# A clamp for the weights' conversion, and five pieces of work put elsewhere in the steps of an attention and gated-product kernel

## The chip, the core and the metric

The kernel runs on one core of a Trainium2 chip. The core has a matrix engine (TensorE, PE in the profile; its weight loads are PEld), a vector engine (VectorE, DVE), a scalar engine (ScalarE, ACT), a general engine (GpSimd, POOL) and a queue engine that here only issues transfers (SyncE, SP). Each engine works through its own list of instructions in order, and waits on semaphores for the others. The metric is the time of one execution on the device in microseconds (us); the median of a few executions is given.

## The reference

```python
# x (8, 8, 512, 64) and state (8, 8, 32, 64) in float32; B, H, S, D = x.shape
scores = scale * x @ state.T                  # per batch and head: 512 x 32
a = softmax(scores);    xread = a @ state     # 512 x 64
scores2 = scale * state @ x.T                 # 32 x 512
a2 = softmax(scores2);  sread = a2 @ x        # 32 x 64
x = concat([xread, sread], axis=2)            # (8, 8, 544, 64)
x = x.transpose(0, 2, 1, 3).reshape(4352, 512)
h = x @ w_in                                  # w_in (512, 2048)
g = h * cos(h)
out = g @ w_out                               # w_out (2048, 512), out (4352, 512) in float32
```

The two weights arrive as 64-bit floating-point numbers, since numpy scaled them by a 64-bit scalar. The kernel has to bring them to 32 bits itself.

## The kernel before

**Tiles and steps.** The 8 batches have 512 token rows each. The work on tokens is cut into 128 steps: step 16b + f takes batch b and columns 128f to 128f + 127 of the hidden width 2048. Sixteen more steps (128 to 143) do all 256 state rows at once. In each step `hidden` (L467) fills a PSUM tile `h` with the hidden values, by two matmuls of 128x128 by 128x512; the profile counts two records for each. The attention is folded in: the left operand is `sw`, the product of state and `w_in` (`products`, L314, copied out of PSUM by `products_kept` on ACT or `products_taken` on DVE, L441), the right one is `aT`, the softmax. `h` comes in units of 2 pi.

**The gate** follows in four instructions. `gate` (L473, ACT) adds a large constant, which rounds; `gate2` (L476, DVE) subtracts it and `h`; `gate3` is Abs (L481, ACT) and Sin (L482, ACT), which gives the cosine; `gate4` (L488, DVE) multiplies with `h` into a slot of `g_all`. There are two `h` tiles, so `hidden` of step k can start only when `gate4` of step k - 2 is done.

**The second product** (`output`, L532) lags three steps behind, four in the first 16 steps. It treats two batches as a pair and uses seven instead of eight block products. For that `w_out` is cut into blocks `a11`, `a12`, `a21`, `a22`, from which POOL makes the sums `s1`, `s2`, `s4` and `s3` (L820; `s3` lies in the place of `a21`), eight instructions in the steps that `block_at` gives. In the second batch of a pair, differences of gated tiles are needed (`minus`, L494): for the first pair all on POOL, for later pairs one a step on DVE and, in the last eight steps of the pair, two on POOL. `s1` is read by outputs of steps 16 to 23, `s2` and `s4` by those of steps 24 to 31, `s3` by the outputs that one pair leaves to the next (`p7`).

**The conversion.** Each weight load (`loads`, 0 to 17, then 18 and 19, which fetch a part of `w_out` anew) goes through `convert_part`: "1" (ACT, L225) takes the high words as float32, without sign and times a power of two, "2" (ACT, L228) makes the three top bits of the low words; "b" (DVE, L231) shifts the former left by three; "c" (DVE, L234) puts the sign in; "d" (POOL, L239) adds the latter; "f" starts a later load on SP. Loads 0 to 3 are 128x512 values, the others 128x1024. `conv_at` gives the step in which "1" and "2" stand; the rest stands in the step after. Within a step the order written in the loop is the order on each engine: after `hidden` come `gate` and `gate2`, then the planned parts `go(1)` (ACT) and `go(3)` (DVE), then the conversions' DVE and POOL part, and "1" if ACT has no planned part; `gate3`; one instruction out of `later` (sums and transposes for the stores, L552, L559, on DVE); `gate4`; then the second halves `go(2)` (ACT) and `go(4)` (DVE) and "2".

**The plan.** `plan(b)` spreads the next batch's attention over a batch's steps: transposed tokens, `scores` (L314), `max1` (L328), `spread1` (L334), `shift` (L351), `max2` (L344), the exponentials (`exps`, L355 and L360, which need another table in ACT), the sums, the normalisation `norm1` (L381), then `turn` (PE, L387) with its eviction `turn_kept` (ACT, L392), `reads` (PE, L404) and `keep` (DVE, L414). `spread`, which `norm1` reads, and `a2T`, which `turn_kept` writes, are the same memory (`xT[:, 0:2]`). Before step 0 a stretch of instructions is written out by hand for batch 0.

Of the kernel before, what the change touches and what calls it, by code (L numbers as in the profile page):

```python
# [10 lines left out]
I32 = mybir.dt.int32  # L11
U32 = mybir.dt.uint32
ALU = mybir.AluOpType
ACTF = mybir.ActivationFunctionType
# [9 lines left out]
def kernel(  # L24
# [8 lines left out]
    nc = tc.nc  # L33
# [10 lines left out]
    scale = 1.0 / math.sqrt(D)  # L44
# [27 lines left out]
    a11, a12 = w_out[:, 0, 0:NH], w_out[:, 0, NH:NF]  # L72
# [3 lines left out]
    s3 = a21  # L76
# [128 lines left out]
    def convert(i, parts):  # L205

        for p in parts:  # L210
            if p == "f":
                if i not in (1, 2) and i + 3 < N_LOADS:
                    fetch(max(i + 4, 6))
            elif f64:
                convert_part(i, p)

    def convert_part(i, p):
        raw, dst = raws[i], loads[i][0]
        bits = dst.bitcast(I32)
# [3 lines left out]
        e = e.bitcast(I32)  # L223
        if p == "1":
            nc.scalar.activation(dst, raw.bitcast(F32)[:, :, :, 1],  # L225
                                 func=ACTF.Abs, scale=2.0 ** -112)
        elif p == "2":
            nc.scalar.activation(e, raw.bitcast(U32)[:, :, :, 0],  # L228
                                 func=ACTF.Copy, scale=2.0 ** -29)
        elif p == "b":  # L230
            nc.vector.tensor_scalar(bits, bits, 3, None,  # L231
                                    op0=ALU.logical_shift_left)
        elif p == "c":
            nc.vector.scalar_tensor_tensor(out=bits, in0=raw[:, :, :, 1],  # L234
                                           scalar=-2 ** 31, in1=bits,
                                           op0=ALU.bitwise_and,
                                           op1=ALU.bitwise_xor)
        else:
            nc.gpsimd.tensor_tensor(bits, bits, e, op=ALU.add)  # L239

# [478 lines left out]
    a0.all_tokens(3, 4)  # L719
    a0.scores()  # L720
    warm(10, acc[SIDE][1])
    convert(0, "12b")
    convert(1, "12")
    a0.max1()
    a0.spread1()
    a0.shift()
# [9 lines left out]
    convert(3, "12")  # L736
    a0.max2()
    a0.exp2()
    convert(2, "bcdf")

# [3 lines left out]
    def plan(b):  # L744
        pe, x_act, y_act, x_dve, y_dve = [
            {s: [] for s in range(NF)} for _ in range(5)]

        def prod(s, b, nt, *bank):
            pe[s].append((b, "products", nt) + bank)
            if b == 1 and nt > 0:  # L750
                x_dve[s].append((b, "products_taken", nt) + bank)
            else:
                x_act[s].append((b, "products_kept", nt) + bank)

        def pairs(s, b, name, kept, i):
            pe[s] += [(b, name, i), (b, name, i + 1)]
            x_act[s].append((b, kept, i))
            y_act[s].append((b, kept, i + 1))

        def early(b, s):  # L760
            if b == 1:
                pairs(s[0], b, "tokens", "tokens_kept", 0)
                pairs(s[1], b, "tokens", "tokens_kept", 2)
            else:
                for k in range(NK):
                    to = (x_dve, y_dve)[k % 2]
                    to[s[k // 2]].append((b, "tokens_turned", k))
            pe[s[2]].append((b, "scores"))
            x_dve[s[2]].append((b, "max1"))
            x_dve[s[3]].append((b, "spread1"))  # L770
            y_dve[s[3]].append((b, "shift"))
            x_dve[s[4]].append((b, "max2"))
            y_act[s[4]].append((b, "exps"))
            x_dve[s[5]].append((b, "sums"))
            y_dve[s[5]].append((b, "spread1"))
            x_dve[s[6]].append((b, "norm1"))

        def late(b, s):
            pairs(s[0], b, "turn", "turn_kept", 0)
            pe[s[1]].append((b, "reads", 0))  # L780
            pe[s[2]].append((b, "reads", 1))
            x_dve[s[2]].append((b, "keep"))
            if len(s) > 3:
                turned(b, s[3])

        def turned(b, s):
            pe[s].append((b, "keep2"))
            x_act[s].append((b, "keep3"))


        if b == 0:
            pe[0].append((0, "products", 0, SIDE, HC, WC))
            y_dve[0] += [(0, "products_taken", 0, SIDE, HC, WC),
                         (0, "inverse2")]
            prod(7, 0, 2, SIDE)
            prod(11, 0, 3)
            prod(13, 1, 0, MAIN)
            late(0, (1, 2, 3, 4))
            early(1, (5, 6, 7, 8, 9, 10, 11))
            late(1, (12, 13, 14))  # L800
        else:
            bank = (SIDE,) if b == 1 else ()
            if b == 1:
                turned(1, 0)
            prod(0, b, 1, *[MAIN for _ in bank])
            prod(4, b, 2, *bank)
            prod(9, b, 3, *bank)
            if b + 1 < B:
                prod(14, b + 1, 0)
                early(b + 1, (1 + (b == 1), 2 + (b == 1), 5, 6, 7, 8, 9))  # L810
                late(b + 1, (10, 11, 12, 15))
        return pe, x_act, y_act, x_dve, y_dve


    conv_at = {s: 4 + i for i, s in enumerate(
        (0, 1, 2, 3, 4, 5, 6, 7, 8, 10, 11, 12, 13, 14))}
    conv_at.update({B * NF + 5: N_LOADS, B * NF + 7: N_LOADS + 1})

    def blocks(op, out_, a, b, r):
        nc.gpsimd.tensor_tensor(out_[:, r], a[:, r], b[:, r], op=op)  # L820

    lo, hi = slice(0, NH // 2), slice(NH // 2, NH)
    block_at = {15: (ALU.add, s1, a21, a22, lo),
                17: (ALU.add, s1, a21, a22, hi),
                18: (ALU.subtract, s2, s1, a11, lo),
                19: (ALU.subtract, s2, s1, a11, hi),
                20: (ALU.subtract, s4, a12, s2, lo),
                21: (ALU.subtract, s4, a12, s2, hi),
                22: (ALU.subtract, s3, a11, a21, lo),
                23: (ALU.subtract, s3, a11, a21, hi)}  # L830
    LAG = 3

    line = []
# [1 line left out]
    for step, t in enumerate(all_tiles):  # L835
        s = step % NF
        if s == 0 and t.b < B:
            steps = plan(t.b)
        todo = [p[s] if t.b < B else [] for p in steps]

        def go(n):
            for p in todo[n]:
                part(*p)

        last, conv = conv_at.get(step - 1, -1), conv_at.get(step, -1)
        if step == B * NF + (0 if f64 else 8):
            fetch(N_LOADS + 2)
        if step == 4:
            warm(1, acc[MAIN][0])
        if step != 1:  # L850
            hidden(t)
        if step == 0:
            hidden(all_tiles[1])
            warm(3, acc[MAIN][0])
            gate(t)
            gate2(t)
            convert(3, "bcdf")
            convert(4, "1")
            go(0)
        else:  # L860
            go(0)
            if step == 5:
                states(1, acc[SIDE][1])
            gate(t)
            gate2(t)
            if step == 3:
                warm(4, acc[MAIN][0])
                part(0, "products", 1, SIDE)
                part(0, "products_kept", 1, SIDE)
            go(1)  # L870
            go(3)
            if step == 1:
                convert(4, "bcdf")
            elif last >= 0:
                convert(last, "bcdf")
            if conv >= 0 and not todo[1]:
                convert(conv, "1")
        gate3(t)
        if later:
            later.pop(0)()  # L880
        gate4(t)
        if conv >= 0 and todo[1] and step > 0:
            convert(conv, "1")
        if t.pair is not None:
            sums(t)
        if step == 6:
            states_kept(1, acc[SIDE][1])
        go(2)
        if conv >= 0:
            convert(conv, "2")  # L890
        go(4)
        if step in block_at:
            blocks(*block_at[step])
        if t.pair is not None:
# [36 lines left out]
```

## Time and profile before

| what | value |
|---|---|
| median of 3 runs (lowest, highest) | 786.97 us (786.81, 787.05) |
| the profiled execution | 786.81 us, its span in the profile 785.0 us |
| busy: PE, DVE, ACT, POOL | 765.1, 417.3, 389.1, 176.7 us |
| TensorE's granted clock | 1.00 in all stretches but the last 5 us |
| PE without a matmul, 0 to 65 us | 5.8 us |
| 65 to 103 us | 5.6 us |
| 103 to 190 us | 2.8 us |
| 190 to 506 us | 1.4 us, in two places |
| 506 to 785 us | 4.3 us, at the end |

The rows for PE without a matmul are the length of a stretch less PE's busy time in it. In a line of the order of time the first number is the start in us from the beginning of the span, the second how long the instruction, or a run of equal ones, was busy; then engine, line, operation, output and inputs with their shapes; in brackets stands how long the engine had been idle and what ended that. Such a run of equal instructions is marked x2, x4 and so on. A DVE instruction of 0.69 us lets the next one start after some 0.60 if that does not need its result.

### The profile page before, as it was taken

The numbers are of one execution on the slowest core, as the hardware profiler recorded it, in microseconds if no ns is written. First come the engines' busy times: TensorE is split into PE (matmuls) and PEld (weight loads), VectorE is DVE, ScalarE is ACT, GpSimd is POOL, SyncE is SP. The second block draws the span as 40 slices with busy tenths as digits, with TensorE's granted clock in tenths as the row PEclk, the third lists the DMA queues.
The fourth block names the chain that finished last, engine by engine and source line by source line (L and its number), as shares of the span: only waits on it lengthen the run. The fifth ranks groups of instructions, "written<-read, shape, count | busy, mean of one in ns | idle before, by whom it ended". The sixth has DMA issues, their size and how long they took to land.

```text
span 785.0 us, 7535 instructions
## 1 busy us (share of the span) xinstructions
PE 765.1 (97%) x2664; PEld 340.3 (43%) x2664; DVE 417.3 (53%) x656; ACT 389.1 (50%) x626; POOL 176.7 (23%) x118
## 2 busy tenths in 40 slices
PE   8998899899999999999999999999999999999997
PEld 3443433344344444444344434434444444455554
DVE  5768778623563466734554467635554446431431
ACT  3888954733463545633473446443563445322222
POOL 2344359673000000641000001640000004610200
PEclk9999999999999999999999999999999999999999
DMA  8595451060011510250104310330100114000021
GB/s 241 167 263 187 141 100 28 4 104 1 3 25 31 102 24 5 34 101 0 24 5 76 58 27 15 54 67 0 28 1 0 28 28 130 4 0 15 13 41 40
DMA packets 161957, 43.49 MB, mean 55 GB/s; under 512 B 153920, under 2 KB 153920, under 8 KB 161920
## 3 DMA queue, kind: packets, MB, share of 16 engines
q1 hardware_dynamic: 161024, 42.49, 24.8%
q10 hardware_dynamic: 768, 0.39, 0.2%
q8 instruction: 21, 0.34, 0.2%
q0 software_dynamic: 128, 0.13, 0.1%
q14 instruction: 16, 0.13, 0.1%
HBM read 34.08 MB, written 8.91 MB: 55 GB/s over the span
## 4 chain that ended last, share of the span: by engine, by line
PE 81%; ACT 10%; DVE 6%; issue 1%; DMA 1%; SPq 0%; POOL 0%; DVEq 0%
PE o L532 44%; PE h L467 26%; PE at L314 4%; PE o L652 4%; PE at L404 2%; ACT q L482 1%; ACT q L481 1%; ACT s L228 1%; DVE q L476 1%; ACT q L473 1%; DVE g_all L488 1%; ACT xT L360 1%; ACT w_in L225 1%; ACT L482 1%; DVE xT L334 1%
## 5 line engine op out<-in xcount | busy, mean ns | idle before, releaser
L467 PE MATMUL h<-aT,sw 128*128 128x512 f32 x512 | 241.5, 594 | 11.0 <-DVE g_all L488 8.1
L532 PE MATMUL o<-g_all,w_out 128*128 128x512 f32 x512 | 236.4, 598 | 1.2 <-POOL w_out L239 1.2
L494 POOL TENSOR_TENSOR g_all<-g_all 128x512 f32<-128x512 f32 x80 | 112.1, 1423 | 451.5 <-DVE g_all L488 447.9
L473 ACT ACTIVATE q<-h 128x512 f32<-128x512 f32 (+1 forms) x144 | 82.1, 570 | 262.3 <-PE h L467 262.2
L476 DVE SCALAR_TENSOR_TENSOR q<-q,h 128x512 f32<-128x512 f32 (+1 forms) x144 | 94.2, 654 | 216.9 <-ACT q L473 216.9
L532 PE MATMUL o<-g_all,s 128*128 128x512 f32 x384 | 177.3, 598 | 0.0
L488 DVE TENSOR_TENSOR g_all<-h,q 128x512 f32<-128x512 f32 (+1 forms) x144 | 94.8, 658 | 124.8 <-ACT q L482 118.6
L467 PEld LDWEIGHTS h<-aT,sw 128*128 128x128 f32 x512 | 96.4, 190 | 135.4 <-issue 110.7
L532 PEld LDWEIGHTS o<-g_all,w_out 128*128 128x128 f32 x512 | 94.0, 190 | 125.5 <-issue 118.4
L481 ACT ACTIVATE q<-q 128x512 f32<-128x512 f32 (+1 forms) x144 | 87.6, 608 | 93.5 <-DVE q L476 93.4
L532 PEld LDWEIGHTS o<-g_all,s 128*128 128x128 f32 x384 | 70.8, 190 | 91.7 <-issue 87.3
L482 ACT ACTIVATE q<-q,halfpi 128x512 f32<-128x512 f32 (+1 forms) x144 | 100.5, 698 | 4.5
L239 POOL TENSOR_TENSOR w_out<-w_out,s 128x1024 int32<-128x1024 int32 x10 | 23.9, 2390 | 77.1 <-DVE w_out L234 73.5
L494 DVE TENSOR_TENSOR g_all<-g_all 128x512 f32<-128x512 f32 x48 | 33.2, 692 | 1.6
L441 ACT COPY sw<-at 128x512 f32<-128x512 f32 x50 | 26.8, 589 | 9.0 <-PE at L314 9.0
L467 PE MATMUL h<-sT,w_in 128*128 128x256 f32 x128 | 30.2, 379 | 0.0
L652 PE MATMUL o<-w_out,g_all 128*128 128x512 f32 x64 | 29.6, 592 | 0.0
L467 PEld LDWEIGHTS h<-sT,w_in 128*128 128x128 f32 x128 | 24.3, 190 | 10.1 <-issue 6.7
L239 POOL TENSOR_TENSOR w_in<-w_in,s 128x1024 int32<-128x1024 int32 (+1 forms) x10 | 19.3, 1929 | 38.8 <-DVE w_in L234 36.5
L314 PE MATMUL at<-w_in,stT 64*32 64x512 f32 x400 | 27.2, 601 | 0.0
L538 DVE SCALAR_TENSOR_TENSOR held<-o,held 128x512 f32<-128x512 f32 x40 | 25.3, 675 | 2.9 <-PE o L532 2.9
L559 DVE STREAM_TRANSPOSE ot<-held 128x512 f32<-128x512 f32 x32 | 22.1, 692 | 0.0
(80 smaller groups left out, 427.7 us busy)
## 6 DMA issues: line engine op xcount, KB each, us to landing
out_dram<-ot SPq DMA_DIRECT2D x132, 64.0 KB, 2.0
g_all<-in_moe_w_out_dram SPq DMA_DIRECT2D x8, 1024.0 KB, 4.9
g_all<-in_moe_w_in_dram SPq DMA_DIRECT2D x6, 1024.0 KB, 5.2
xT<-in_x_dram SPq DMA_DIRECT2D x96, 64.0 KB, 2.3
x_b<-in_x_dram SPq DMA_DIRECT2D x24, 256.0 KB, 4.6
x_b<-in_x_dram SPq DMA_DIRECT2D x16, 128.0 KB, 4.0
g_all<-in_moe_w_in_dram SPq DMA_DIRECT2D x4, 512.0 KB, 6.0
x_b<-in_moe_w_out_dram SPq DMA_DIRECT2D x1, 1024.0 KB, 5.9
```

Of the source, the lines that this page charges most:

```text
L239: nc.gpsimd.tensor_tensor(bits, bits, e, op=ALU.add)
L314: nc.tensor.matmul(out=(to or at)[j][Ns * k:Ns * k + Ns, 0:n], lhsT=w[D * j:D * j + D, self.b, Ns * k:Ns * k + Ns], rhs=r(slice(D * j, D * ...
L441: (copy or nc.scalar.copy)(sw_of[self.b, nt][:, j, c0:c1], to[j][:, 0:c1 - c0])
L467: nc.tensor.matmul(out=t.hp, lhsT=t.lhs(i), rhs=t.rhs(i), start=(i == 0), stop=(i == t.kn - 1))
L473: nc.scalar.activation(t.q, t.hp, func=ACTF.Copy, bias=MAGIC)
L476: nc.vector.scalar_tensor_tensor(out=t.q, in0=t.q, scalar=MAGIC, in1=t.hp, op0=ALU.subtract, op1=ALU.subtract)
L481: nc.scalar.activation(t.q, t.q, func=ACTF.Abs)
L482: nc.scalar.activation(t.q, t.q, func=ACTF.Sin, bias=halfpi, scale=-TWO_PI)
L488: nc.vector.tensor_tensor(t.g, t.hp, t.q, op=ALU.mult)
L494: engine.tensor_tensor(out, a, b, op=ALU.subtract)
L532: nc.tensor.matmul(out=acc[bank][ch], lhsT=w[:, i, P * ch:P * ch + P], rhs=g.g, start=(i == 0), stop=(i == NH - 1))
L652: nc.tensor.matmul(out=acc[MAIN][i], lhsT=t.g[:, P * i:P * i + P], rhs=w_out[:, :, t.f, :], start=(t.n_th == 0), stop=(t.n_th == NF - 1))
```

## The change

- **A clamp.** "1" takes the absolute value alone. A new part "a" raises every value to at least 2^-15, in place: on DVE, for load 1 on POOL. It stands ahead of "b" everywhere. "2" writes the bits as a float32 between 2 and a little above, whose bit pattern also holds the exponent's offset that the power of two gave before. So every load has one instruction more.
- **Conversions.** Loads 13 to 17 are converted one step later: "1" and "2" in steps 11 to 15 instead of 10 to 14.
- **Step 3.** The eviction of the second part of batch 0's `sw` stands on ACT behind Abs and Sin instead of ahead of them.
- **Step 25.** The last of batch 1's `products` is copied by ACT (`products_kept`) and not by DVE.
- **Normalisation.** For batches 2 to 7 `norm1` stands behind `gate4` of its step, not ahead. That is steps 25, 41, 57, 73, 89 and 105.
- **Stores.** Where DVE has a planned part in a step (`todo[3]`), the instruction out of `later` comes behind `gate4` and "2" and not ahead of `gate4`.
- **Block sums.** The first six are a step later (16, 18 to 22); the two of `s3` are in steps 32 and 33.

PE's list is the same. The line numbers of the changed kernel are two higher from the conversion to the loop (L381 becomes L383), and "a" stands at L231.

```diff
         if p == "1":
             nc.scalar.activation(dst, raw.bitcast(F32)[:, :, :, 1],
-                                 func=ACTF.Abs, scale=2.0 ** -112)
+                                 func=ACTF.Abs)
         elif p == "2":
             nc.scalar.activation(e, raw.bitcast(U32)[:, :, :, 0],
-                                 func=ACTF.Copy, scale=2.0 ** -29)
+                                 func=ACTF.Copy, scale=2.0 ** -51, bias=2.0)
+        elif p == "a":
+            engine = nc.gpsimd if i == 1 else nc.vector
+            engine.tensor_scalar(dst, dst, 2.0 ** -15, None, op0=ALU.max)
...
-            nc.gpsimd.tensor_tensor(bits, bits, e, op=ALU.add)
+            nc.gpsimd.tensor_tensor(bits, bits, e.bitcast(I32), op=ALU.add)
...
-    convert(0, "12b")
-    convert(1, "12")
+    convert(0, "12ab")
+    convert(1, "12a")
...
-    convert(2, "bcdf")
+    convert(2, "abcdf")
+    convert(3, "a")
...
-            if b == 1 and nt > 0:
+            if b == 1 and 0 < nt < 3:
                 x_dve[s].append((b, "products_taken", nt) + bank)
             else:
                 x_act[s].append((b, "products_kept", nt) + bank)
...
-            x_dve[s[6]].append((b, "norm1"))
+            (x_dve if b == 1 else y_dve)[s[6]].append((b, "norm1"))
...
     conv_at = {s: 4 + i for i, s in enumerate(
-        (0, 1, 2, 3, 4, 5, 6, 7, 8, 10, 11, 12, 13, 14))}
+        (0, 1, 2, 3, 4, 5, 6, 7, 8, 11, 12, 13, 14, 15))}
...
-    block_at = {15: (ALU.add, s1, a21, a22, lo),
-                17: (ALU.add, s1, a21, a22, hi),
-                18: (ALU.subtract, s2, s1, a11, lo),
-                19: (ALU.subtract, s2, s1, a11, hi),
-                20: (ALU.subtract, s4, a12, s2, lo),
-                21: (ALU.subtract, s4, a12, s2, hi),
-                22: (ALU.subtract, s3, a11, a21, lo),
-                23: (ALU.subtract, s3, a11, a21, hi)}
+    block_at = {16: (ALU.add, s1, a21, a22, lo),
+                18: (ALU.add, s1, a21, a22, hi),
+                19: (ALU.subtract, s2, s1, a11, lo),
+                20: (ALU.subtract, s2, s1, a11, hi),
+                21: (ALU.subtract, s4, a12, s2, lo),
+                22: (ALU.subtract, s4, a12, s2, hi),
+                32: (ALU.subtract, s3, a11, a21, lo),
+                33: (ALU.subtract, s3, a11, a21, hi)}
...
-            convert(4, "1")
+            convert(4, "1a")
...
                 part(0, "products", 1, SIDE)
-                part(0, "products_kept", 1, SIDE)
...
-                convert(last, "bcdf")
+                convert(last, "abcdf")
...
         gate3(t)
-        if later:
+        if step == 3:
+            part(0, "products_kept", 1, SIDE)
+        if later and not todo[3]:
             later.pop(0)()
         gate4(t)
...
         if conv >= 0:
             convert(conv, "2")
+        if later and todo[3]:
+            later.pop(0)()
         go(4)
```

More of the change, by code (lines that the diff above doesn't have):

```diff
@@ L222, in convert_part @@
         e = low[i % 2][:, c0:c0 + m * w].rearrange("p (m f) -> p m f", m=m)
-        e = e.bitcast(I32)
         if p == "1":
             nc.scalar.activation(dst, raw.bitcast(F32)[:, :, :, 1],
-                                 func=ACTF.Abs, scale=2.0 ** -112)
+                                 func=ACTF.Abs)
         elif p == "2":
             nc.scalar.activation(e, raw.bitcast(U32)[:, :, :, 0],
-                                 func=ACTF.Copy, scale=2.0 ** -29)
+                                 func=ACTF.Copy, scale=2.0 ** -51, bias=2.0)
+        elif p == "a":
+            engine = nc.gpsimd if i == 1 else nc.vector
+            engine.tensor_scalar(dst, dst, 2.0 ** -15, None, op0=ALU.max)
         elif p == "b":
```

## The prediction

> **What bounds the kernel now.** I read the busy times, then the stretches, then PE's waits, then the order of time around each.
>
> ```profile
> PE 765.1 (97%) x2664; PEld 340.3 (43%) x2664; DVE 417.3 (53%) x656; ACT 389.1 (50%) x626; POOL 176.7 (23%) x118
> ```
>
> TensorE is the bound: only 20 us of the span of 785.0 are without a matmul. The stretches say where (time; PE, PEld, DVE, ACT, POOL busy; clock; DMA):
>
> ```profile
> 65.00:103.00 38.00, 32.41 (x135) 13.66 (x133) 30.37 (x46) 34.45 (x49) 14.81 (x7) 1.00 0.53 158
> 190.00:317.00 127.00, 127.00 (x435) 53.59 (x435) 72.74 (x116) 62.92 (x102) 0.00 (x0) 1.00 0.17 29
> ```
>
> From 190 to 317 us PE never stops, so a move of other engines' work costs nothing there. From 65 to 103 us ACT is busy 34.45 and DVE 30.37 of 38 us: there the weights are converted, and DVE work can reach PE. PE's stalls, in order of time (start, busy, what, in brackets the idle time and who ended it):
>
> ```profile
> 45.13 1.98 PE L532 MATMUL o<-g_all,w_out 128*128 128x512 f32 x4 [1.16 <-POOL w_out L239]
> ...
> 76.10 1.98 PE L467 MATMUL h<-aT,sw 128*128 128x512 f32 x4 [1.95 <-DVE g_all L488]
> ...
> 83.45 1.98 PE L467 MATMUL h<-aT,sw 128*128 128x512 f32 x4 [2.43 <-ACT sw L441]
> ...
> 102.99 1.98 PE L467 MATMUL h<-aT,sw 128*128 128x512 f32 x4 [1.21 <-DVE g_all L488]
> ...
> 151.69 1.98 PE L467 MATMUL h<-aT,sw 128*128 128x512 f32 x4 [0.97 <-DVE g_all L488]
> ...
> 322.76 1.98 PE L467 MATMUL h<-aT,sw 128*128 128x512 f32 x4 [0.71 <-DVE g_all L488]
> ```
>
> Each L467 pass waits for the gate's product (L488) of two steps earlier, or for an eviction. These passes are my milestones: "pass k" opens step k. Passes 4, 11, 12, 16, 18, 27 start at 41.98, 76.10, 83.45, 102.99, 113.00, 151.69; pass 59 at 322.76; pass 91 is its twin (493.83, idle 0.70). The last view is the normalisation (L381) with its neighbours:
>
> ```profile
> 148.94 2.10 DVE L381 TENSOR_TENSOR aT<-aT,xT 128x1024 f32<-128x1024 f32 x1
> ...
> 151.11 0.59 ACT L392 COPY xT<-at 128x512 f32<-128x512 f32 x1 [1.39 <-PE o L532]
> ```
> ```profile
> 317.41 3.02 POOL L494 TENSOR_TENSOR g_all<-g_all 128x512 f32<-128x512 f32 x2 [132.12 <-DVE g_all L488]
> ...
> 319.71 1.80 DVE L381 TENSOR_TENSOR aT<-aT,xT 128x1024 f32<-128x1024 f32 x1
> ...
> 324.68 1.10 PE L404 MATMUL at<-x_b,xT 128*64 128x128 f32 x16
> ```
>
> L381 takes 1.21 us in the rows that meet no POOL work; issued inside a POOL subtraction it took 2.10 and 1.80, its end being 1.21 us after a point 0.12 us ahead of the recorded end of the POOL instruction. So it waits for POOL. And L392, the eviction that overwrites `xT[:, 0]`, waits for L381, which reads it as `spread`: 151.11 is 0.07 us after L381's end (PE, which the row names, had long been done). PE's L404 needs L392.
>
> **Part 1: the clamps and the moved conversions.** Twenty clamps are added: loads 0, 2, 3 (128x512) and 4 to 19 (128x1024) on DVE, load 1 on POOL. No row shows this form. The bounds are the shift L231, also SBUF to SBUF with a constant (0.42 and 0.69 us), and the two-input L234 (0.69 and 1.23). I take L231, the nearest in form: 0.45 and 0.73 us from issue to issue, as the shift waits for its input (15.04 to 15.49, 51.43 to 52.16).
>
> The Trainium skill, "VectorE: DVE Perf Modes", section on the perf-mode tier table, gives fp32 scalar operations from SBUF twice the rate of two-input ones, 1227 ns for 2048 elements. My estimate from it for 1024 elements is 0.69 us; at the normal rate it would be 1.23, and part 1 some 3 us dearer.
>
> To pass 4: load 0's clamp stands before the score maximum, whose chain PE waits for at 21.28: +0.45. Load 1's lies in POOL's idle 12.55 us (between 0.29, the 128x128 select, and 1.27, its 128x512 addition). Those of loads 2 to 4 fit into DVE's idle 1.01 and 1.85 us before 24.60 and 28.20, unless POOL's additions hold them up: 0 to +0.5. Load 5's comes after the gate at 34.91; POOL's addition behind it ended at 39.97, and step 3's product waited for it: +0.73. So pass 4 is 1.2 to 1.7 late. The 1.16 us at 45.13 stay, since load 6 moves as well. Step 3's eviction behind Sin fills ACT's idle 2.37 us before 41.14 with Abs and Sin (1.36 us); the eviction still waits for its product, but ACT is earlier afterwards, which removes PE's 0.54 us at 54.55 (at worst nothing). Pass 7: +0.65 to +1.2.
>
> Steps 7 to 9: DVE runs without a gap from 66.12 to 76.04. Load 10's clamp makes that start 0.75 to 1.4 late (it uses up the idle 0.47), and loads 11 and 12 add 2 x 0.73: pass 11 +2.2 to +2.85. Behind these DVE queues step 9's product.
>
> Step 10 loses conversion 13. The exponentials have only one of the two clamps before them: +1.47 to +2.1. ACT loses load 13's second pass before the eviction at 82.81 (1.0 from issue to issue) and 0.2 of delay to Abs. Pass 12: +0.3 to +0.9; the stall of 2.43 shrinks accordingly.
>
> Steps 11 to 16 carry the five conversions a step later, each with a clamp. ACT's two passes of load 13 now follow Sin in step 11; step 12's gate starts 1.3 late, step 14's 1.35. PE has cover until pass 16, where it idled 1.21 already; the clamp of step 14 makes this +2.0 to +2.6. In step 16 the three DVE operations of load 17 (0.73 + 0.73 + 1.23) now lie between L441 and the gate's product; PE has two outputs (3.70 us) as cover. Pass 18: +2.0, or +3.0 if a clamp falls into POOL's addition, as the shift at 103.45 did (1.82 instead of 0.69). PE has no idle time from there to 144, so nothing is given back. Load 17's DMA is issued late too (SP: 91.6 to about 98.6, landing 4.9 us, first read about 104), just in time. **Part 1: +2.0 to +3.0, I take +2.6**, nearer the top as two of ten w_out shifts met POOL.
>
> **Part 2: step 25.** The two DVE copies (1.27 us) go to ACT, which idled 2.00 us there; L381 goes behind the product. The product moves from 150.96 to about 149.3 (Sin then limits), so pass 27 is bound by PE, 150.72: **-1.0**. L381 is issued as POOL's batch ends (149.95) and ends about 151.2, where it ended before, so L392 is no later. Bounds: -1.0 to +2, the latter if POOL's next three subtractions go first.
>
> **Part 3: steps 57 and 89.** The product is only 0.2 us earlier (Sin limits; the store's transpose still precedes it), so PE gains 0.15 of the 0.71. L381 now follows the product and DVE's subtraction L494 (322.75) and meets POOL's two subtractions, issued at 322.79. Those took 3.02 instead of 2 x 1.27 because the first waited for L494; its start works out at 0.06 us before DVE's next instruction. So POOL comes first, and L381, asking since 323.2, gets in 0.12 us ahead of the first's recorded end (324.37), before the second is issued (0.04 ahead of such an end elsewhere). It ends at 325.5, L392 at 326.1, and L404 starts at 326.1 instead of 324.68: +1.45. Behind L392 queue Abs and Sin of step 58, behind L381 gate2; their product ends near 328.1, before pass 60 asks (330.7). Bounds: +0.4 if L381 is let in first (L392 then ends at 325.05), +2.7 if both subtractions precede it (L392 then ends at 327.35). **Two such steps: +2.9** (0.8 to 5.4).
>
> The Trainium skill, "SBUF — State Buffer", summary of rules, says that of a two-input VectorE operation and a GpSimd one the second to issue blocks fully until the first finishes. It speaks against this move; by it the price is the same +1.45 a step, as it counts one subtraction.
>
> **Nothing for the rest.** In steps 41, 73 and 105 L381 moves too, but PE's L404 comes 4.8 us after L392 (236.66 to 242.09), against 1.2 us. The block sums of steps 15 to 21 come a step later on POOL, their first readers (pass 19's outputs on) 2 us or more behind them; without that cover one costs up to 2.37. The last two, in steps 32 and 33, find POOL idle from 190 on, with their reader three steps away. The store steps behind the product change DVE's order where PE never idles. Loads 18 and 19 are clamped after 730 us, DVE a third busy.
>
> **Sum.** 2.6 - 1.0 + 2.9 = +4.5 on the profiled execution's 786.81 (span 785.0 plus 1.8), which lies 0.16 below the median 786.97: 791.3 there, 791.5 as median.
>
> **Rivals.**
> - The other side: the moved L381 wins and the clamps hide. Place: the three stalls before passes 27, 59, 91 go (0.97 + 0.71 + 0.70 = 2.4): 784.6. It decides if part 1 stays under 0.8. For it: DVE idles 2.02 and 2.00 us before gates in steps 2 and 3. Against: DVE's unbroken run up to 76.04.
> - No measurable change: part 1 at its low end, L381 let in at once: 2.0 - 1.0 + 0.8 = +1.8, or less if steps 14 to 16 absorb a clamp: 788.0.
> - L381 let in first but part 1 as taken: 2.6 - 1.0 + 0.8: 789.4.
> - Both subtractions go first: 2.6 - 1.0 + 5.4: 794.0. For it: POOL's pairs follow each other without a gap in every row.
> - Clamps at 1.23: +3.2 over the six on the path: 794.7.
>
> **How the numbers follow.** Forecast 0.42, rivals in order 0.08, 0.12, 0.18, 0.14, 0.06. A measurement can tell about 0.2%, 1.6 us, from no change. The range 787.6 to 795.5 leaves out the first rival and the ends of others. Faster 0.08, same 0.12, slower 0.80.
>
> **What would show it.** Right: PE's stall before pass 11 near 3, before pass 12 below 2; pass 18 near 115.6; no idle before pass 27; L381 of 2.3 us or so after pass 59, with PE waiting 1.5 for ACT's copy before the reads of steps 59 and 91. Wrong: clamps of 1.2 us, L381 of 1.2 or 3.5 in step 57, or a wait for load 17's DMA.

## The result and the profile after

| | before | after |
|---|---|---|
| median (lowest, highest), 6 runs each on one chip | 787.01 us (786.81, 788.56) | 791.68 us (791.36, 794.97) |
| profiled execution | 786.81 us | 791.47 us |
| its span | 785.0 us | 789.7 us |

The ratio is 1.0066, with an interval from 1.0047 to 1.0085: slower by 4.7 us, where 4.5 were forecast (791.5, range 787.6 to 795.5).

The busy times on the page of the changed kernel, and two stretches of its trace (limits and length; PE, PEld, DVE, ACT and POOL busy; clock; DMA):

```profile
PE 766.0 (97%) x2664; PEld 339.9 (43%) x2664; DVE 429.4 (54%) x673; ACT 390.6 (49%) x628; POOL 181.4 (23%) x119
```
```profile
65.00:103.00 38.00, 33.78 (x136) 14.05 (x134) 31.20 (x47) 32.42 (x47) 11.85 (x5) 1.00 0.39 137
190.00:317.00 127.00, 127.00 (x436) 53.59 (x434) 71.67 (x114) 61.72 (x99) 1.48 (x1) 1.00 0.17 29
```

PE does the same work; its idle time grew. DVE has 17 instructions more (19 clamps, less the two copies that went to ACT) and is 12 us busier. Between 190 and 317 us PE still never stops. The stalls of PE, from the order of time (start, busy, what; in brackets the idle time and who ended it):

```profile
60.83 0.66 PE L316 MATMUL o<-w_in,stT 64*32 64x512 f32 x7 [0.40 <-DVE stT L148]
...
72.45 1.98 PE L469 MATMUL h<-aT,sw 128*128 128x512 f32 x4 [0.89 <-DVE g_all L490]
...
78.82 1.98 PE L469 MATMUL h<-aT,sw 128*128 128x512 f32 x4 [2.67 <-DVE g_all L490]
...
84.22 1.98 PE L469 MATMUL h<-aT,sw 128*128 128x512 f32 x4 [0.48 <-ACT sw L443]
...
105.44 1.99 PE L469 MATMUL h<-aT,sw 128*128 128x512 f32 x4 [2.43 <-DVE g_all L490]
```

The stall ahead of pass 11 grew from 1.95 to 2.67 and a new one of 0.89 stands ahead of pass 10; ahead of pass 12 it shrank from 2.43 to 0.48, ahead of pass 16 it grew from 1.21 to 2.43. The steps around the moved normalisation, in the same view:

```profile
152.68 1.22 DVE L383 TENSOR_TENSOR aT<-aT,xT 128x1024 f32<-128x1024 f32 x1
152.90 5.83 POOL L496 TENSOR_TENSOR g_all<-g_all 128x512 f32<-128x512 f32 x4 [0.15 <-DVE g_all L490]
153.36 1.88 PE L469 MATMUL h<-aT,sw 128*128 128x512 f32 x4
...
319.54 0.70 DVE L561 STREAM_TRANSPOSE ot<-held 128x512 f32<-128x512 f32 x1
320.17 1.20 DVE L336 STREAM_TRANSPOSE xT<-i 128x1024 f32<-128x1024 f32 x1
321.29 0.65 DVE L478 SCALAR_TENSOR_TENSOR q<-q,h 128x512 f32<-128x512 f32 x1
...
324.13 1.98 PE L469 MATMUL h<-aT,sw 128*128 128x512 f32 x4 [0.52 <-DVE g_all L490]
324.16 3.99 POOL L496 TENSOR_TENSOR g_all<-g_all 128x512 f32<-128x512 f32 x2 [2.17 <-DVE g_all L490]
324.72 2.29 DVE L383 TENSOR_TENSOR aT<-aT,xT 128x1024 f32<-128x1024 f32 x1
327.09 0.58 ACT L394 COPY xT<-at 128x512 f32<-128x512 f32 x1 [3.25 <-PE h L469]
327.73 1.09 PE L406 MATMUL at<-x_b,xT 128*64 128x128 f32 x16 [1.61 <-ACT xT L394]
```

In step 25 the normalisation L383 takes its free time, 1.22, and pass 27 (153.36) has no wait any more. In step 57 it takes 2.29: it asks at 324.72, while POOL has two subtractions to do, and POOL's pair lasts 3.99. The copy L394, which overwrites what L383 reads, follows 0.08 us after its end (PE, which the row names, had long been done), and PE waits 1.61 us for it. A stall of 0.52 ahead of pass 59 stays, where 0.71 stood before. The three lines from 319.54 on matter for that below.

How late each pass starts against the kernel before, in the two profiles:

| pass | forecast | measured |
|---|---|---|
| 4 | +1.2 to +1.7 | +1.60 |
| 7 | +0.65 to +1.2 | +0.82 |
| 11 | +2.2 to +2.85 | +2.73 |
| 12 | +0.3 to +0.9 | +0.78 |
| 16 | +2.0 to +2.6 | +2.44 |
| 18, 20 | +2.0 to +3.0 | +2.59, +2.81 |
| 26 to 28 | -1.0 | -1.24 (+2.80 to +1.56) |
| 58 to 60, 90 to 92 | +1.45 each | +1.49, +1.48 |
| 92, to the end | +4.5 | +4.53 |

Nothing moves between 28 and 58, 60 and 90, or after 92. Of each lateness that is counted from the start (passes 4 to 20 and the end), 0.25 is no effect of the change: in this execution the first weights landed later, so that ACT's first read of them is at 10.22 us and not at 9.97. Without it pass 7 is 0.57 late, just below its range, and the others stay in theirs.

### The profile page after: what moved, and what is told of

Its sections match the earlier page's. It is cut to its first block, busy times and chain, and to the rows that moved or that the text cites. A ratio compares the mean times of both kernels' runs of the same rounds, so it can differ in the third digit from the quotient of the medians.

```text
span 789.7 us, 7553 instructions
## 1 busy us (share of the span) xinstructions
PE 766.0 (97%) x2664; PEld 339.9 (43%) x2664; DVE 429.4 (54%) x673; ACT 390.6 (49%) x628; POOL 181.4 (23%) x119
## 4 chain that ended last, share of the span: by engine, by line
PE 81%; ACT 8%; DVE 7%; issue 2%; DMA 1%; POOL 1%; SPq 0%; ACTq 0%; DVEq 0%; POOLq 0%
PE o L534 44%; PE h L469 26%; PE at L316 4%; PE o L654 3%; DVE q L478 2%; PE at L406 2%; ACT q L483 1%; ACT q L484 1%; DVE g_all L490 1%; ACT q L475 1%; ACT xT L362 1%; ACT s L227 1%; DVE xT L336 1%; ACT aT L357 1%; ACT L484 1%
## 5 line engine op out<-in xcount | busy, mean ns | idle before, releaser
L496 POOL TENSOR_TENSOR g_all<-g_all 128x512 f32<-128x512 f32 x80 | 114.8, 1457 | 445.1 <-DVE g_all L490 444.6
L478 DVE SCALAR_TENSOR_TENSOR q<-q,h 128x512 f32<-128x512 f32 (+1 forms) x144 | 94.0, 653 | 202.4 <-ACT q L475 202.4
L490 DVE TENSOR_TENSOR g_all<-h,q 128x512 f32<-128x512 f32 (+1 forms) x144 | 95.1, 661 | 132.4 <-ACT q L484 126.5
L561 DVE STREAM_TRANSPOSE ot<-held 128x512 f32<-128x512 f32 x32 | 22.5, 702 | 0.0
```

The costliest lines, as they stand in the source:

```text
L478: nc.vector.scalar_tensor_tensor(out=t.q, in0=t.q, scalar=MAGIC, in1=t.hp, op0=ALU.subtract, op1=ALU.subtract)
L490: nc.vector.tensor_tensor(t.g, t.hp, t.q, op=ALU.mult)
L496: engine.tensor_tensor(out, a, b, op=ALU.subtract)
```

## The experiments

Shifts of passes below are differences of pass starts between two profiles, less the difference at pass 0, which starts between 21.28 and 22.93 us. Part of that difference is the landing of the first weights: ACT's first read of them is at 9.97 us in the kernel before and at 10.11 to 10.58 in the others. Part of it is load 0's clamp, so that the shifts leave this clamp out: from that read to pass 0 it takes 11.68 to 11.72 us in seven executions with clamps and 11.30 and 11.32 in two without, 0.4 more, near the +0.45 of the prediction. (The other four, at 11.90 to 12.48, have a stretch of half clock at about 8 us.) One more thing must be known to read the times: in ten of the eleven executions profiled below PE's granted clock fell to half for 3.41 us after one to three of the stalls (shown at the store experiment); where such a stretch moved the passes, I say by how much.

### The normalisation in steps 57 and 89

**norm1 ahead of the product again there, behind it in step 25 only.**

```diff
-            (x_dve if b == 1 else y_dve)[s[6]].append((b, "norm1"))
+            (y_dve if b == 2 else x_dve)[s[6]].append((b, "norm1"))
```

> The changed kernel with the normalisation behind the gate's product in step 25 alone, ahead of it everywhere else. My theory (the normalisation, queued behind the product and one POOL subtraction, holds up ACT's copy and so PE's reads): the two idle times of 1.6 us before the reads of steps 59 and 91 go, the normalisation meets at most the end of POOL's work (1.2 to 1.8 us instead of 2.29), the idle 0.5 us before passes 59 and 91 stay because Sin ends last; 1.7 us saved at each place: 788.2 us. Rival (what costs there is the store's transpose behind the product, which makes the spread and the gate of step 57 late): the 1.6 us stay, 791.5 us.

Measured: 789.32 us, ratio to before 1.0019 (1.0009 to 1.0028), the profiled execution 788.24. From its order of time:

```profile
321.93 1.21 DVE L383 TENSOR_TENSOR aT<-aT,xT 128x1024 f32<-128x1024 f32 x1
...
324.20 1.98 PE L469 MATMUL h<-aT,sw 128*128 128x512 f32 x4 [0.52 <-DVE g_all L490]
...
326.12 1.09 PE L406 MATMUL at<-x_b,xT 128*64 128x128 f32 x16
```

L383 is short again and L406 waits for nothing: 3.2 us of the profiled execution come back, as that theory had it (1.7 at each place; the median of the ten executions lies 1.1 above the profiled one). So the two steps are the place of that loss. The stall of 0.52 stays, though norm1 stands where it stood.

**norm1 behind the product but ahead of DVE's own subtraction.** A sixth list of parts, called between `gate4` and `minus`:

```diff
-            (x_dve if b == 1 else y_dve)[s[6]].append((b, "norm1"))
+            (x_dve if b == 1 else z_dve if b in (4, 6) else y_dve)[
+                s[6]].append((b, "norm1"))
...
         gate4(t)
+        go(5)
```

> The changed kernel with the normalisation of steps 57 and 89 still behind the gate's product, but ahead of DVE's own subtraction, so that it is issued about 0.15 us before POOL's first subtraction. My theory (who asks first gets the port and keeps it for the instruction): the normalisation takes 1.21 us, ends about 1.8 us earlier, ACT's copy ends before PE needs it, the 1.6 us before the reads go: 788.5 us. Rival (POOL goes first whenever it has such work, or the place behind the product is itself too late): the normalisation takes 2.3 us or more, or takes 1.2 and PE still waits 0.5 to 1.6 us: 789.5 to 791.7 us.

Measured: 792.35 us, ratio 1.0054 (1.0038 to 1.0069).

```profile
326.33 1.22 DVE L383 TENSOR_TENSOR aT<-aT,xT 128x1024 f32<-128x1024 f32 x1
...
326.49 2.18 POOL L496 TENSOR_TENSOR g_all<-g_all 128x512 f32<-128x512 f32 x1 [2.17 <-DVE g_all L490]
327.46 1.76 DVE L496 TENSOR_TENSOR g_all<-g_all 128x512 f32<-128x512 f32 x1
...
332.26 2.21 PE L534 MATMUL o<-g_all,s 128*128 128x512 f32 x4 [0.87 <-ACT held L545]
```

Asked for first, L383 is free (1.22) and POOL's subtraction waits for it (2.18 instead of 1.27); then DVE's own subtraction waits for POOL (1.76 instead of 0.69). L406 no longer waits, but the gate of the next step is late and PE waits 0.87 at an output instead, so from pass 58 to pass 60 it loses 1.16 where the changed kernel loses 1.49: only 0.33 is won in each step. My 788.5 had left out that second wait. The profiled execution (793.18) also has a start 1.0 later than the changed kernel's and a stretch of half clock ahead of pass 17. That stretch costs 1.6 at pass 17 and 1.3 from pass 20 on, as the changed kernel itself loses 0.36 between these passes and a PE that comes late does not. Without both it would stand at about 790.8, an estimate from these differences.

**norm1 ahead there, and the store's transpose held back only in steps whose DVE part is norm1.** The change holds it back wherever DVE has a planned part, in step 56 too (the sums).

```diff
-            (x_dve if b == 1 else y_dve)[s[6]].append((b, "norm1"))
+            (y_dve if b == 2 else x_dve)[s[6]].append((b, "norm1"))
...
-        if later and not todo[3]:
+        held_back = any(w[1] == "norm1" for w in todo[3])
+        if later and not held_back:
...
-        if later and todo[3]:
+        if later and held_back:
```

> The changed kernel with norm1 ahead of the gate's product again in steps 57 and 89 and the store's instruction behind it only in steps whose DVE part is norm1. Theory: the stall of 0.52 us that the changed kernel keeps ahead of passes 59 and 91 comes from the store's transpose of step 56 and 88, which the change puts behind the gate's product and so ahead of spread1 and of gate2 of the next step; with it back ahead, that stall falls below 0.2, and L406 does not wait: against the changed kernel -2.0 a step, 787.4 in the end. Rival (the stall comes from norm1 ahead of the product): the stall is 0.5 or more, 788.2.

Measured: 787.93 us, ratio 1.0008 (0.9999 to 1.0017).

```profile
318.79 0.65 DVE L561 STREAM_TRANSPOSE ot<-held 128x512 f32<-128x512 f32 x1
...
319.77 0.69 DVE L490 TENSOR_TENSOR g_all<-h,q 128x512 f32<-128x512 f32 x1 [0.33 <-ACT q L484]
...
321.11 1.24 DVE L336 STREAM_TRANSPOSE xT<-i 128x1024 f32<-128x1024 f32 x1
322.27 0.65 DVE L478 SCALAR_TENSOR_TENSOR q<-q,h 128x512 f32<-128x512 f32 x1
...
325.30 1.98 PE L469 MATMUL h<-aT,sw 128*128 128x512 f32 x4
```

In step 56 the transpose L561 now runs while DVE waits for Sin, and 0.33 of idle time is left. So gate2 (L478) of step 57, behind L336, starts 1.56 after pass 58; in the changed kernel, with L561 ahead of both, it was 2.15. What is left of the stall ahead of pass 59 is 0.12, too short for the row to name a releaser. So that stall belongs to the store's transpose of step 56, not to norm1. From pass 58 to 60, and from 90 to 92, it is 2.1 less than in the changed kernel, where 2.0 was expected.

### The clamps and what goes with them

**The clamps alone, on the kernel before** (with the constants in "1" and "2" that belong to them).

```diff
+        elif p == "a":
+            engine = nc.gpsimd if i == 1 else nc.vector
+            engine.tensor_scalar(dst, dst, 2.0 ** -15, None, op0=ALU.max)
...
-                convert(last, "bcdf")
+                convert(last, "abcdf")
```

> The kernel before with the twenty clamps alone; all orders as before. My theory (the clamps lengthen the chain of DVE and ACT that PE waits for in steps 0 to 18): pass 4 is 1.2 to 1.6 us late, pass 11 2.7 to 3.3, pass 12 2.0 to 2.6 since the conversion of load 13 still lies before the copy, pass 18 about 3: 790.0 us (789.3 to 791). Rival (the loss up to step 18 comes from converting the last five loads one step later, and the clamps lie in idle time): passes 12 and 18 within 0.5 us of before, 787.2 us.

Measured: 791.39 us, ratio 1.0044 (1.0029 to 1.0059); the rival falls, and the theory's 790.0 was too low by 1.4. **The change without the clamps** (the same lines taken out of it):

> The changed kernel without the clamps (the scaled absolute value of before); all orders as in the changed kernel. My theory: passes 4 and 11 within 0.5 us of before or earlier, pass 12 about 1.5 us earlier than before, pass 18 0 to 1 us earlier, then 1.1 us won at step 25 and 1.5 lost at each of steps 57 and 89: 788.0 us (787.4 to 788.9). Rival (the later conversions make the loss up to step 18): pass 18 2 us late or more, 790.5 to 791.7 us.

Measured: 789.13 us, ratio 1.0017 (1.0007 to 1.0028); the rival falls, as pass 18 is not late. A half-clock stretch ahead of pass 17 puts its later passes off by 1.6, which the last column leaves out at the end.

| against before, less pass 0 | the change | clamps alone | without clamps |
|---|---|---|---|
| pass 4 | +0.96 | +0.96 | 0.00 |
| pass 8 | +0.32 | +1.79 | -1.40 |
| pass 11 | +2.09 | +3.55 | -1.39 |
| pass 12 | +0.14 | +2.80 | -2.36 |
| pass 16 | +1.80 | +3.85 | -1.69 |
| end | +3.89 | +3.83 | +0.05 |

The two columns add up to that of the change within 0.4 everywhere. The clamps cost 3.85 from pass 0 to pass 16 (a half-clock stretch from 81.6 to 85.0 us may be in passes 12 to 15), and 4.2 with load 0's, which lies ahead of pass 0. The companions give back 1.7 by pass 16: more than I had thought, so that I had put the clamps alone too low. The stall of 1.61 in steps 57 and 89 is there without the clamps as well.

The clamps' own rows in the changed kernel's order of time:

```profile
12.35 1.49 POOL L231 TENSOR_SCALAR w_in<-w_in 128x512 f32<-128x512 f32 x1 [8.47 <-ACT w_in L224]
...
36.38 0.69 DVE L231 TENSOR_SCALAR w_in<-w_in 128x1024 f32<-128x1024 f32 x1
...
105.89 1.82 DVE L231 TENSOR_SCALAR w_out<-w_out 128x1024 f32<-128x1024 f32 x1
```

**Step 3's eviction ahead of Abs and Sin again.**

```diff
                 part(0, "products", 1, SIDE)
+                part(0, "products_kept", 1, SIDE)
...
-        if step == 3:
-            part(0, "products_kept", 1, SIDE)
```

> The changed kernel, but step 3's eviction stands ahead of Abs and Sin again, as before the change. Theory (from the run without clamps, where the lateness fell by 1.4 us from pass 4 to pass 8): the place behind Sin is worth 1.4 us, because ACT, which everything from step 4 to 8 waits for, no longer idles ahead of that eviction. Then pass 8 comes about 1.4 us later than in the changed kernel, with a stall of PE ahead of it, the lateness stays to the end, and the time is about 793.0. Rival (the prediction's): it is worth only the one stall of 0.54 us, 792.2.

Measured: 794.7 us, ratio 1.0082 (1.0053 to 1.0111), two executions; the profiled one has a half-clock stretch ahead of pass 17. The stalls up to pass 8, and the second of them in the kernel before:

```profile
56.27 0.65 PE L271 MATMUL at<-ident,x_b 128*128 128x128 f32 x4 [0.51 <-ACT xT L280]
...
62.46 0.66 PE L316 MATMUL o<-w_in,stT 64*32 64x512 f32 x7 [1.12 <-DVE stT L148]
```
```profile
59.87 0.66 PE L314 MATMUL o<-w_in,stT 64*32 64x512 f32 x7 [0.26 <-DVE stT L148]
```

Pass 7 is 0.75 later than in the changed kernel, pass 8 1.47, pass 16 1.53. The first line is the stall of 0.5 that I had counted. The second stall, 0.26 before, is 1.12 here, 1.11 with the clamps alone and 0.40 in the changed kernel: the clamps lengthen it and the eviction's new place shortens it again. The end is 2.8 later, 1.5 without the 1.3 that such a stretch ahead of pass 17 leaves. The eviction's place is worth 1.5 us, not 0.54.

**Loads 13 to 17 in the steps of before.**

```diff
-        (0, 1, 2, 3, 4, 5, 6, 7, 8, 11, 12, 13, 14, 15))}
+        (0, 1, 2, 3, 4, 5, 6, 7, 8, 10, 11, 12, 13, 14))}
```

> The changed kernel with loads 13 to 17 converted in the steps of before, 10 to 14. Theory: moving them one step later only moves lateness about; here the exponentials of step 10 have two clamps ahead of them again, so pass 12 starts about 2.0 us later than before the change, 1.2 later than in the changed kernel; from pass 18 on the two are within 0.5 us. Time about 792.0. Rival (the later conversions, whose last one comes just ahead of its reader, are themselves a loss): pass 18 at least 1 us earlier than in the changed kernel, time 790.7 or less.

Measured: 792.72 us (791.72 to 794.15; the profiled one 791.72), ratio 1.0070 (1.0045 to 1.0096). Pass 12 is 1.23 later than in the changed kernel, pass 16 0.60, pass 20 and the end 0.24; the rival falls. The later conversions move lateness from one stall to the next and gain a quarter of a microsecond between the two profiles, less than the executions of one kernel differ by.

**The clamps of loads 11 and 12 made twice.**

```diff
-            engine.tensor_scalar(dst, dst, 2.0 ** -15, None, op0=ALU.max)
+            for _ in range(2 if i in (11, 12) else 1):
+                engine.tensor_scalar(dst, dst, 2.0 ** -15, None, op0=ALU.max)
```

> The changed kernel with the clamps of loads 11 and 12 made twice each, which changes no value. Theory: in steps 7 to 9 DVE runs without a gap, so that each instruction in there puts pass 11 off by its own length, 0.73 us: pass 11 1.46 us later than in the changed kernel. The exponentials of step 10 have one of the two clamps ahead of them: pass 12 0.73 later, and the end some 0.7 later, 792.4. Rival (the lateness comes from waits for POOL's additions and not from DVE's own length): pass 11 less than 0.5 us later, end within 0.3.

Measured: 792.22 us, ratio 1.0053 (1.0031 to 1.0076). The doubled rows (their lines are up to three higher than before the change) and what follows:

```profile
68.91 1.53 DVE L232 TENSOR_SCALAR w_in<-w_in 128x1024 f32<-128x1024 f32 x2
...
76.12 1.42 DVE L232 TENSOR_SCALAR w_out<-w_out 128x1024 f32<-128x1024 f32 x2
...
79.44 0.68 DVE L491 TENSOR_TENSOR g_all<-h,q 128x512 f32<-128x512 f32 x1
...
80.18 2.87 PE L470 MATMUL h<-aT,sw 128*128 128x512 f32 x4 [3.40 <-DVE g_all L491]
```

Pass 11 is 1.48 later than in the changed kernel, twice 0.73, and the stall ahead of it 3.40 instead of 2.67. The end is 0.8 later, one clamp. An instruction put into DVE's unbroken run of steps 7 to 9 is paid in full at pass 11; the exponentials of step 10 have only one of the two ahead of them, and that one is what is left at the end. (Right behind that stall PE's four records take 2.87 instead of 1.98, at half clock; that put pass 12 off by a further 1.7, which was gone by pass 16.)

### What I had counted as nothing

**Block sums and stores as before the change.**

```diff
-    block_at = {16: (ALU.add, s1, a21, a22, lo),
+    block_at = {15: (ALU.add, s1, a21, a22, lo),
...
-        if later and not todo[3]:
+        if later:
...
-        if later and todo[3]:
-            later.pop(0)()
```

> The changed kernel with the block sums and the stores' steps as before the change. Theory: both are hidden, every pass within 0.3 us of the changed kernel, time 791.5 to 791.9. Rival (the later block sums keep POOL from the weights' additions less, or more, in steps 15 to 23): pass 16 or 18 moves by 0.5 us or more.

Measured: 792.95 us, ratio 1.0064 (1.0041 to 1.0087), with the start 0.57 later and a half-clock stretch ahead of pass 17. The theory misses; the rival's mark is met, though DVE and not an addition is what POOL holds up: pass 18 is 2.05 later than in the changed kernel. From its order of time:

```profile
112.76 2.80 POOL L823 TENSOR_TENSOR s<-w_out 128x1024 f32<-128x1024 f32 x1
113.39 2.72 DVE L233 TENSOR_SCALAR w_out<-w_out 128x1024 int32<-128x1024 int32 x1
...
117.47 0.69 DVE L490 TENSOR_TENSOR g_all<-h,q 128x512 f32<-128x512 f32 x1
...
118.22 1.98 PE L469 MATMUL h<-aT,sw 128*128 128x512 f32 x4 [0.39 <-DVE g_all L490]
...
326.06 1.98 PE L469 MATMUL h<-aT,sw 128*128 128x512 f32 x4
...
329.65 1.09 PE L406 MATMUL at<-x_b,xT 128*64 128x128 f32 x16 [1.61 <-ACT xT L394]
```

The block sum of step 15 (L823) is on POOL when the shift of load 17 is issued, and the shift takes 2.72 instead of 0.69. From 105.89 to the gate's product that pass 18 waits for (L490, end 118.16) DVE is never idle for more than 0.1 us, so this product is 2.0 late whenever PE comes. PE lost 1.6 to half clock ahead of pass 17, but inside that wait: only 0.39 of it is left as a stall. So the later block sums gain 1.9 (pass 20); this follows from the rows, and no execution of this kernel without the half-clock stretch was profiled. In the kernel before, the same block sum (109.00 to 111.36) met no shift, since load 17's was at 103.45: its later place is worth this only beside the later conversions. With the stores as before there is no stall ahead of passes 59 and 91, and each comes 0.59 earlier: the stores' new rule costs 1.2 in all. Together, the two gain the changed kernel 0.8 us, which is what the end is later by here.

Its stretches of 1 us show the clock (the number before the last two):

```profile
105.00:106.00 1.00, 0.00 (x0) 0.00 (x0) 0.97 (x3) 0.77 (x1) 0.60 (x1) 1.00 1.46 128
106.00:107.00 1.00, 0.97 (x2) 0.49 (x3) 1.00 (x2) 0.40 (x1) 1.00 (x1) 0.88 1.39 124
107.00:108.00 1.00, 1.00 (x2) 0.33 (x1) 1.00 (x1) 0.97 (x3) 0.75 (x1) 0.50 1.45 123
108.00:109.00 1.00, 1.00 (x3) 0.23 (x1) 0.97 (x2) 1.00 (x1) 0.00 (x0) 0.50 1.23 132
109.00:110.00 1.00, 1.00 (x10) 0.23 (x16) 0.97 (x2) 0.80 (x3) 0.00 (x0) 0.50 0.89 114
```

Behind the stall of 1.97 us that ends at 106.03 the clock is 0.50 from 106.76 on, for 3.41 us, and pass 16 to pass 17 takes 8.20 us instead of 6.58.

### Only the parts that gain

Step 3's eviction behind Sin, step 25's copies and normalisation, and the store's narrow rule, on the kernel before; in a second version the later conversions and block sums too.

```diff
-            if b == 1 and nt > 0:
+            if b == 1 and 0 < nt < 3:
...
-            x_dve[s[6]].append((b, "norm1"))
+            (y_dve if b == 2 else x_dve)[s[6]].append((b, "norm1"))
...
-        if later:
+        if step == 3:
+            part(0, "products_kept", 1, SIDE)
+        held_back = any(w[1] == "norm1" for w in todo[3])
+        if later and not held_back:
...
+        if later and held_back:
+            later.pop(0)()
```

> The kernel before, with only those parts of the change that the runs so far found to gain: step 3's eviction behind Sin; in step 25 the last product copied by ACT and norm1 behind the gate's product; and the store's instruction behind the gate's product only in the steps whose DVE part is norm1 (the change puts it behind in step 56 too, where it holds up spread1 and gate2 of step 57). Conversions in steps 10 to 14, no clamps. Theory: pass 8 -1.4 us against before, pass 27 a further -1.0, passes 59 and 91 a further -0.5 to -0.7 each, as the stall of 0.7 ahead of them goes: 783 to 784, faster than both kernels. Rival: what is gained up to pass 8 is lost again in the stalls ahead of passes 12 and 16, 785.0.

> The same, with loads 13 to 17 converted a step later (steps 11 to 15) and the block sums in the later steps. Theory (from the run of the change without clamps): pass 12 -2.3 us against before, pass 18 -1.7, pass 27 -2.8, passes 59 and 91 -0.5 to -0.7 each: 782.8, some 0.3 ahead of the kernel with the conversions in steps 10 to 14. Rival: the later conversions cost what they gain, the two are within 0.2 of each other.

Measured: the first 784.80 us (783.48 to 786.46), ratio 0.9966 (0.9955 to 0.9977); the second 785.71 (783.09 to 787.69), ratio 0.9978 (0.9969 to 0.9988). Both beat the kernel before, by 0.3 and 0.2%, and with it the changed one. The first one's passes, against before and less pass 0: -1.37 at pass 8, -1.33 at 26, -2.57 at 28, -3.16 at 59, -3.76 at 91, each step as expected; the rival's loss at passes 12 and 16 does not come. (The median is 0.8 above the time I gave; the start was 1.5 later in the profiled execution.) Its profile:

```profile
150.70 1.88 PE L467 MATMUL h<-aT,sw 128*128 128x512 f32 x4
...
321.08 1.99 PE L467 MATMUL h<-aT,sw 128*128 128x512 f32 x4
...
322.99 1.09 PE L404 MATMUL at<-x_b,xT 128*64 128x128 f32 x16
```

No wait stands ahead of passes 27 and 59 or the reads. The second version is 0.26 ahead of the first at pass 16, but its profiled execution has two stretches of half clock that cost 1.6 and 1.7 us, the second one behind the stall of 1.86 ahead of pass 26, which the kernel before has without it:

```profile
148.00:149.00 1.00, 1.00 (x2) 0.31 (x2) 0.13 (x1) 0.80 (x2) 1.00 (x2) 0.50 0.00 0
149.00:150.00 1.00, 1.00 (x4) 0.55 (x3) 0.42 (x1) 0.86 (x2) 1.00 (x2) 0.50 0.00 0
```

Which of the two is better is not settled by these times.

## Why the prediction was right, and where it was not

- **PE as the bound, and the stretch without effect: right.** No pass moved between 28 and 58 or after 92. The forecast of +4.5 met a profiled difference of 4.66, of which 0.25 is the landing of the weights; that the sum is so close is in part luck, as the next points say.
- **The price of a clamp: right.** 0.42 and 0.69 us on DVE, the values of the shift. The estimate from the Trainium skill, "VectorE: DVE Perf Modes", section on the perf-mode tier table, was 0.69, and the rows agree. POOL's clamp was not bounded rightly: 1.49 us, above the end of 1.27; it lay in idle time. Load 0's clamp cost 0.4 ahead of pass 0 (+0.45).
- **DVE's unbroken run up to pass 11: right and shown** by the doubled clamps, +1.48 for two. The clamp of load 16 met POOL's addition at 105.89 (1.82 us), as the upper value for pass 18 had it.
- **Step 3's eviction: mis-sized, and hidden by a second error.** "Removes PE's 0.54 us" is the term; it measured 1.5. What I had not named is the stall ahead of pass 8, which the clamps lengthen from 0.26 to 1.1 and the eviction's new place shortens again to 0.40. The two errors cancel, by luck: the start of DVE's run, put at 0.75 to 1.4 late, measured 1.13 (67.25 against 66.12). The clamps by themselves cost 4.2 where part 1 as a whole came to +2.8, or about +2.6 without the landing of the weights (I took +2.6).
- **Step 25: right,** -1.24 against -1.0. L383 was not held up: it started 0.2 ahead of POOL's next batch. No run moves the copies or norm1 alone, so which of the two brings this is not shown.
- **Steps 57 and 89: right as a sum, +1.5 each, wrong in one part.** L383's wait (2.29 us, let in after the first of POOL's two subtractions) and the delay of the reads (L404, now L406) are as worked out: they start at 327.73, or 326.17 without the 1.56 by which pass 58 is late, against the forecast 326.1. But "the store steps behind the product change DVE's order where PE never idles" was wrong. PE does idle, ahead of passes 59 and 91: the store's transpose of step 56 puts gate2 of step 57, and with it Sin, 0.6 us back. That is also why "the product is only 0.2 us earlier (Sin limits)" came out (4.25 us after pass 58 instead of 4.48). Sin does limit, but with the stores as before it lets the product come 0.8 earlier (3.65 after pass 58) and the stall of 0.7 is gone; the sum would then have been about 3.3, 4.5 less 1.2. So the 0.15 that I let the move gain was right by luck.
- **"Nothing for the rest": wrong for the stores (+1.2),** and for the block sums right only because they were moved too: in their old steps beside the later conversions they put pass 18 off by 2.0.
- **Rivals.** Both of POOL's subtractions first would have made L383 3.5 us, let in first 1.2; it was 2.29. In the order tried ahead of DVE's subtraction it was let in first, and PE then waited elsewhere.
- **The later conversions** hardly bear on the end (0.24), as the sum of part 1 implied; no wait for load 17 appeared.

The Trainium skill, "SBUF — State Buffer", summary of rules, says that of a two-input VectorE operation and a GpSimd one the second to issue waits for the first. The rows of step 57 agree in both directions (L383 2.29 behind POOL; POOL 2.18 behind L383). They add what came here when POOL had a second instruction queued: the one that waits goes next, ahead of it (POOL's pair takes 3.99 with L383 in its middle, 3.01 without). One-input operations of DVE waited for POOL here too: the shift of 2.72 for the block sum, the clamp of 1.82 for an addition.

## What to carry to other kernels

Price an added instruction by whether its engine's unbroken run ends in a wait of the bound engine: there it costs its whole length, and a stall further on gives back only as much as it had. A vector operation moved next to another engine's queue of port-holding work was delayed here by one of these instructions, and so was whatever overwrites what it reads. A rule that moves work "behind the product" has to be read in every step where it takes hold: with norm1 ahead of the product it gained 0.6 us in step 57 and lost 0.4 of that by step 56, and in the changed kernel, where norm1 stands behind and the rule does not reach step 57, only the loss is left. A stretch of low clock may be taken off a measured time only where PE was the bound behind it: ahead of pass 18 of the store experiment it hid a wait of 2.0 us.

## What the runs showed of the hardware that I had not expected

- **Half clock after short stalls.** The granted clock fell to 0.50 for 3.41 us each time behind stalls of PE of 1.9 to 3.4 us, in some executions and not in others (0.88, 0.50, 0.50, 0.50 above; none behind the stalls of 2.43 and 2.67 in the profiles of before and after). Such a stretch cost up to 1.7 us, and nothing where a stall further on took it up. The Trainium skill, "TensorE: Matmul & The Clock Gate", Part 1, tells of a free-running window of some 3.4 us of idleness that halves the clock. The length agrees, and a free-running window would explain why it is not in every execution; but the stalls here, except one of 3.40, are much shorter than such a window, and PE's stretches were not wholly idle for that long. I did not test it. It fits that the executions of the changed kernel that took 793.68 and 794.97 us had a mean granted clock of 0.993 and 0.991, the other four 0.998 to 1.000.
- **POOL's one-input clamp is dearer than its two-input addition:** 1.49 against 1.28 us for 128x512 (one clamp in each run, always of 1.49; the clamp is in float32, the addition in int32; DVE's clamp took 0.42).
- **The start varies:** pass 0 lay between 21.28 and 22.93 us, a range a third as large as the whole effect. The landing of the weights makes up to 0.6 of it and load 0's clamp 0.4; the four latest starts are the four executions with a stretch of half clock at about 8 us.
